# Retention and soft mixture of experts on one core: all stages rebuilt, with steps in pairs, rows of 4 to 8 KB and an order by hand on every engine

## The chip, the cores and the metric

One core of a Trainium2 chip runs the kernel. The metric is the device time of one execution in microseconds (us), lower being better: 169.63 us, the median of 3 runs (169.53 to 170.11). All data are float32.

## The reference

Retention over 4 batches, 8 heads, 768 tokens and head width 64 makes x (3072 x 512). A layer with 8 experts of 4 slots each (`phi` 512 x 32, `w1` 8 x 512 x 1024, `w2` 8 x 1024 x 512) makes the result.

```python
for t in range(S):                                   # retention, scale = 1/8
    state = gamma * state + outer(k[t], v[t])
    y[t] = scale * q[t] @ state
x = y, tokens by (head, width)
logits = x @ phi
d = softmax of logits over all 3072 tokens;  slot_input = d.T @ x
slot_out[e] = relu(slot_input[e] @ w1[e]) @ w2[e]
c = softmax of logits over the 32 slots;     result = c @ slot_out
```

The softmax over all tokens divides the kernel in two: no slot input is known before the last token's logits are.

## The kernel before, in words

**Retention, 24 steps of 128 tokens.** A step is one chunk of one batch, and a batch's six chunks follow each other. `load_kq` and `load_vk` bring a step's keys and queries turned (head width on partitions) and its values and keys untouched, 512 KB each in rows of 4 KB, into slots of one ring of 48. POOL scales the values by a power of gamma (L169). PE makes `scores` (L182, a pair of heads in the two halves of the rows), DVE masks them (L187, four pieces of 256 columns). `attend` adds the products with the carried state (L202) and with the values (L207) in PSUM, and DVE scales the sum into `yT` (L213, four pieces). `state` adds keys times values (L226), and ACT copies the state out (L228). `natural` turns `yT` back on PE (L234; ACT copies, L235). After every fourth step PE makes that group's logits (L245, 32 columns for each of four steps), and in the steps after it `dispatch_p`, `dispatch_u` (L278, L287) and `combine_weights` (L303) run.

**Experts.** After the last group a chain of small operations makes the slot inputs `siT` (L430). `hidden` (L445) multiplies them by `w1` in 16 units of four products, one expert in each quarter of PE's columns; `hidden_t` turns the result. Then L537 multiplies by `w2` in three blocks of 256, 128 and 128 output columns. `finish` copies a block's sum out (L500), spreads it (L504), splits it in two (L506, L507) and multiplies by the combine weights (L519, 512 tokens at a time); DVE and ACT copy the products (L525, L522), and each 512 KB leaves by L523. The blocks before are finished in between the units of the next.

**Order.** PE's order is the program's (`ORDERED`); the other engines are set by the scheduler. SP issues all DMAs on one queue, in program order. Weights are 64 loads of 512 KB: 34 are spread over the 24 steps (`NPRE`), the rest follow as slots come free.

Of the kernel before, what the change touches and what calls it, by code (L numbers as in the profile page):

```python
# [17 lines left out]
C = 128  # L18
# [10 lines left out]
WARM = 5  # L29
# [31 lines left out]
def constants():  # L61
    g = 1.0 - 2.0 ** (-5.0 - np.arange(H, dtype=np.float64))
    p = np.arange(128)
    k = np.zeros((128, K_ALL), np.float64)
    k[:, K_MASK:K_MASK + 128] = p[None, :] >= p[:, None]
    t = (np.arange(NC)[None, :, None] * C + p[:, None, None]).astype(np.float64)
    k[:, K_VSC:K_VSC + 48] = (g[None, None, :] ** -t).reshape(128, 48)
    k[:, K_ID:K_ID + 128] = np.eye(128)
    gp = g[head_of(p[:, None] // 64, np.arange(NPAIR)[None, :])]
    k[:, K_YB:K_YB + 24] = (gp[:, None, :] ** (np.arange(NC)[None, :, None] * C)).reshape(128, 24)  # L70
    k[:, K_J:K_J + GRP] = (p[:, None] // NSLOT) == np.arange(GRP)[None, :]
    k[:, K_YT:K_YT + 64] = (gp[:, :, None] ** (8 * np.arange(16)) / np.sqrt(D)).reshape(128, 64)
# [5 lines left out]
def retention_soft_moe_kernel(  # L78
    ctx: ExitStack,
    tc: tile.TileContext,  # L80
    kq_in: bass.AP,
    vk_in: bass.AP,
    phi: bass.AP,
    w1: bass.AP,
    w2: bass.AP,
    consts: bass.AP,
# [37 lines left out]
    weights = [("w1", 4 * g + j, k) for g in range(2) for k in range(NK) for j in range(4)]  # L124
    for cb, (_, w) in enumerate(BLOCKS):
        for g in range(2):
            if w == 64:
                weights += [("w2", 4 * g + 2 * j, cb) for j in range(2)]
            else:
                weights += [("w2", 4 * g + j, cb) for _ in range(NFC // FPS[w]) for j in range(4)]  # L130

    def load_weights(n):
        for _ in range(n):
            if not weights:
                return
            which, e, k = weights.pop(0)
            t = slot()
            if which == "w1":
                nc.sync.dma_start(t, w1[e, k * 128:(k + 1) * 128, :])
                w1t[e, k] = t  # L140
            else:
                n = 1024 if BLOCKS[k][1] == 64 else FPS[BLOCKS[k][1]] * BLOCKS[k][1]
                nc.sync.dma_start(t[:, 0:n], w2[w2n[0]:w2n[0] + 128 * n].rearrange("(p n) -> p n", n=n))
                w2n[0] += 128 * n
                if BLOCKS[k][1] == 64:
                    w2t[e, k], w2t[e + 1, k] = [t[:, 0:512]], [t[:, 512:1024]]
                else:
                    w2t.setdefault((e, k), []).append(t)

    st = {}  # L150

    def load_kq(i):
        t = slot()
        nc.sync.dma_start(t, kq_in[i])
        st[i] = dict(kT=t[:, 0:512].rearrange("p (g t) -> p g t", t=C),
                     qT=t[:, 512:1024].rearrange("p (g t) -> p g t", t=C))

    def load_vk(i):
        t = slot()
        v = t[:, 0:512].rearrange("p (h e) -> p h e", e=D)  # L160
        st[i].update(v=v, kn=t[:, 512:1024].rearrange("p (h e) -> p h e", e=D))
        if i % NC == NC - 1:
            nc.sync.dma_start(t[:, 0:512], vk_in[i, :, 0:512])
        elif i == 0:
# [4 lines left out]
        nc.gpsimd.tensor_tensor(v, v, vsc[:, i % NC, :].unsqueeze(2).broadcast_to([128, H, D]), ALU.mult)  # L169

    def scores(i):
        s = st[i]
        if i == 0:
            sc = [[ps.tile([128, 2, C], F32, name=n, bufs=2 if n == "sm" else 1) for n in t]
                  for t in (("sc0", "sc1"), ("sm", "sm"))]
        else:
            full = [ps.tile([128, NPAIR, C], F32, name=f"sc{r}") for r in range(2)]
            sc = [[f[:, 2 * hf:2 * hf + 2] for f in full] for hf in range(2)]
# [12 lines left out]

    def attend(i):
        s = st[i]
        c = i % NC
        y = [ps.tile([128, 2, C], F32, name=f"y{b}") for b in range(2)]
        if c > 0:
            for gl in range(2):
                for b in range(2):
                    g = 2 * b + gl
                    for r in range(2):  # L200
                        sl, o = slice(r * D, (r + 1) * D), half_of(r, g) * D
                        nc.tensor.matmul(y[b][o:o + D, gl, :], sst[sl, g, :], s["qT"][sl, g, :],  # L202
                                         start=(gl == 0), stop=False, skip_group_check=True)
        for g in range(NPAIR):
            for r in range(2):
                o = half_of(r, g) * D
                nc.tensor.matmul(y[g // 2][o:o + D, g % 2, :], s["v"][:, 2 * g + r, :], s["A"][:, r, g, :],  # L207
                                 start=(c == 0 and g % 2 == 0), stop=True, skip_group_check=True)
# [21 lines left out]
    def natural(i):  # L230
        s = st[i]
        xp = ps.tile([128, DM], F32, name="xp")
        for g in range(NPAIR):
            nc.tensor.transpose(xp[:, g * 128:(g + 1) * 128], s["yT"][:, g, :], ident)  # L234
        (nc.vector.tensor_copy if i == NSTEP - 1 else nc.scalar.copy)(s["xn"], xp)  # L235
# [13 lines left out]

    def logits(g):  # L250
# [349 lines left out]
```

## Time and profile before

| | |
|---|---|
| time, median of 3 runs | 169.63 us |
| span of the profiled execution | 168.4 us (1.2 us under the median; all sums below start from this execution) |
| PE busy | 153.6 us, 91% |
| DVE, ACT, POOL busy | 93.6, 42.0, 30.5 us |
| moved by DMA | 64.62 MB (64.26 by the kernel's queue), mean 384 GB/s |

The page divides the span in 40 slices. Each shows the busy share of the engines, the clock granted to TensorE (PEclk) and the rate of the DMA engines, so a stage that starves the queue shows as a dip in GB/s. A PE that is "busy" can still be one that works at the pace of its inputs: the chain of waits tells which came last.

### The profile page before, as it was taken

To read this page: it belongs to the slowest core of one execution; us is meant where nothing else is said; L and a number is where in the kernel's file an instruction comes from. 1 tells how busy PE (TensorE), PEld (TensorE's weight loads), DVE (VectorE), ACT (ScalarE), POOL (GpSimd) and SP (SyncE) were. 2 spreads that over 40 slices of the span, in tenths; PEclk is the share of its full clock that TensorE was granted. 3 is DMA by queue.
4 is the path that set the end of the run, shared out by engine and by line. 5 is a ranking of instruction groups with operands and counts; after the bars stand their busy time and mean duration, and the time that the engine had idled before them with its cause. 6 is when DMAs were issued, how large, how long until landed. Compare 5 with 4: busy or idle time off the path is not lost.

```text
span 168.4 us, 5648 instructions
## 1 busy us (share of the span) xinstructions
PE 153.6 (91%) x2370; PEld 109.6 (65%) x2370; DVE 93.6 (56%) x299; ACT 42.0 (25%) x104; POOL 30.5 (18%) x40
## 2 busy tenths in 40 slices
PE   8699779999999999999989799999999999999940
PEld 2577667687868786888678578867432546666620
DVE  0576445596677876694777566984223121355550
ACT  3022213232423141323212232315202030043330
POOL 0252222230304122232223221300050000000000
PEclk9999999999999999999999999999999999999998
DMA  6999999999999999999999999999999999969966
GB/s 185 324 416 411 408 402 415 401 410 406 410 407 406 407 409 406 408 409 404 407 407 411 405 409 406 403 384 367 378 312 404 415 412 406 412 263 397 384 266 263
DMA packets 18458, 64.62 MB, mean 384 GB/s; under 512 B 2048, under 2 KB 2432, under 8 KB 18432
## 3 DMA queue, kind: packets, MB, share of 16 engines
q1 hardware_dynamic: 18432, 64.26, 97.4%
q8 instruction: 19, 0.31, 0.8%
q14 instruction: 7, 0.06, 0.1%
HBM read 57.96 MB, written 6.29 MB: 381 GB/s over the span
## 4 chain that ended last, share of the span: by engine, by line
PE 50%; DMA 40%; DVE 3%; SPq 2%; issue 1%; DVEq 0%
DMA r<-in_kq_dram 18%; DMA r<-in_w_dram 18%; PE sc L537 9%; PE sc L182 6%; PE y L445 4%; PE y L207 4%; DMA r<-in_vk_dram 4%; PE xp L234 3%; PE sm L245 3%; PE y L202 3%; PE xp L445 2%; PE S L445 2%; PE sm L287 2%; PE S L226 2%; PE sm L519 2%; PE sm L331 1%
## 5 line engine op out<-in xcount | busy, mean ns | idle before, releaser
L187 DVE TENSOR_TENSOR r<-sc,kt 128x256 f32<-128x256 f32 x94 | 33.3, 417 | 17.1 <-PE sc L182 16.1
L169 POOL TENSOR_TENSOR r<-r,kt 128x512 f32<-128x512 f32 x24 | 25.1, 1044 | 75.5 <-DMA r<-in_vk_dram 51.1
L213 DVE SCALAR_TENSOR_TENSOR r<-y,kt,ysc 128x128 f32<-128x128 f32 x96 | 27.7, 343 | 9.6 <-PE y L207 6.7
L182 PE MATMUL sc<-r 64*128 64x128 f32 x376 | 27.4, 284 | 4.4 <-DMA r<-in_kq_dram 4.1
L207 PE MATMUL y<-r 128*64 128x128 f32 x384 | 27.3, 280 | 2.6 <-POOL r L169 2.4
L182 PEld LDWEIGHTS sc<-r 64*128 64x128 f32 x376 | 23.1, 187 | 7.3 <-issue 4.0
L207 PEld LDWEIGHTS y<-r 128*64 128x64 f32 x384 | 21.3, 136 | 7.3 <-POOL r L169 3.8
L235 ACT COPY r<-xp 128x512 f32<-128x512 f32 x23 | 13.5, 586 | 42.9 <-PE xp L234 33.3
L234 PE MATMUL xp<-kt,r 128*128 128x128 f32 x96 | 16.5, 287 | 0.1
L537 PE MATMUL sc<-r 128*32 128x128 f32 (+1 forms) x384 | 15.9, 310 | 0.0
L234 PEld LDWEIGHTS xp<-kt,r 128*128 128x128 f32 x96 | 10.6, 141 | 7.0 <-DVE r L187 3.4
L537 PEld LDWEIGHTS sc<-r 128*32 128x32 f32 x384 | 10.6, 110 | 6.0 <-issue 2.9
L228 ACT COPY sst<-S 128x256 f32<-128x256 f32 x20 | 7.5, 373 | 27.6 <-PE S L226 27.5
L202 PE MATMUL y<-r,sst 64*64 64x128 f32 x320 | 13.3, 282 | 0.0
L226 PE MATMUL S<-r 128*64 128x64 f32 x320 | 13.1, 222 | 0.0
L226 PEld LDWEIGHTS S<-r 128*64 128x64 f32 x320 | 12.3, 138 | 0.0
L202 PEld LDWEIGHTS y<-r,sst 64*64 64x64 f32 x320 | 8.5, 132 | 3.3 <-issue 2.1
L445 PE MATMUL y<-r,siT 128*32 128x512 f32 x64 | 8.2, 597 | 0.0
L245 PE MATMUL sm<-r,phis 128*32 128x128 f32 x192 | 7.3, 276 | 0.0
L245 PEld LDWEIGHTS sm<-r,phis 128*32 128x32 f32 x192 | 5.4, 109 | 1.4 <-issue 1.0
L313 POOL TENSOR_TENSOR cnat<-cnat,cz 128x128 f32<-128x128 f32 x6 | 2.4, 401 | 17.5 <-DVE cz L312 14.5
L287 PE MATMUL sm<-r,p 128*32 128x512 f32 x40 | 5.3, 605 | 0.0
(112 smaller groups left out, 124.2 us busy)
## 6 DMA issues: line engine op xcount, KB each, us to landing
r<-in_w_dram SPq DMA_DIRECT2D x64, 512.0 KB, 10.1
r<-in_kq_dram SPq DMA_DIRECT2D x24, 512.0 KB, 10.1
r<-in_vk_dram SPq DMA_DIRECT2D x19, 512.0 KB, 10.1
out_dram<-r SPq DMA_DIRECT2D x12, 512.0 KB, 4.3
r<-in_vk_dram SPq DMA_DIRECT2D x6, 256.0 KB, 9.6
kt<-in_consts_dram SPq DMA_DIRECT2D x1, 136.0 KB, 3.1
kt<-in_consts_dram SPq DMA_DIRECT2D x1, 78.0 KB, 5.6
phis<-in_phi_dram SPq DMA_DIRECT2D x1, 64.0 KB, 6.2
```

What stands on the lines that cost most here:

```text
L169: nc.gpsimd.tensor_tensor(v, v, vsc[:, i % NC, :].unsqueeze(2).broadcast_to([128, H, D]), ALU.mult)
L182: nc.tensor.matmul(sc[g // 2][r][:, g % 2, :], s["kT"][sl, g, :], s["qT"][sl, g, :], start=True, stop=True)
L187: nc.vector.tensor_tensor(A[:, r, 2 * hf:2 * hf + 2], sc[hf][r], mask.unsqueeze(1).broadcast_to([128, 2, C]), ALU.mult)
L202: nc.tensor.matmul(y[b][o:o + D, gl, :], sst[sl, g, :], s["qT"][sl, g, :], start=(gl == 0), stop=False, skip_group_check=True)
L207: nc.tensor.matmul(y[g // 2][o:o + D, g % 2, :], s["v"][:, 2 * g + r, :], s["A"][:, r, g, :], start=(c == 0 and g % 2 == 0), stop=True, sk ...
L213: nc.vector.scalar_tensor_tensor(yT[:, g, :], y[g // 2][:, g % 2, :], ybs[:, c, g:g + 1], ysc[:, g, :], ALU.mult, ALU.mult)
L226: nc.tensor.matmul(S_[r * D:(r + 1) * D, g, :], s["kn"][:, 2 * g + r, :], s["v"][:, 2 * g + r, :], start=(c == 0 and g == 0), stop=True, s ...
L234: nc.tensor.transpose(xp[:, g * 128:(g + 1) * 128], s["yT"][:, g, :], ident)
L235: (nc.vector.tensor_copy if i == NSTEP - 1 else nc.scalar.copy)(s["xn"], xp)
L245: nc.tensor.matmul(q["ltp"][32 * j:32 * j + 32, :], phis[:, p, :], st[GRP * g + j]["yT"][:, p, :], start=(p == 0), stop=(p == NPAIR - 1), ...
L445: nc.tensor.matmul(hp[g][half][32 * j:32 * j + 32, :], siT[:, k, :], w1t[4 * g + j, k][:, half * 512:(half + 1) * 512], start=(k == 0), st ...
L537: nc.tensor.matmul(op[32 * j:32 * j + 32, :w], hT[fc // 4][:, fc % 4, 4 * g + j, :], t[:, f * w:(f + 1) * w], start=(g == 0 and fc == 0), ...
```

## The change

Steps are now ordered chunk by chunk with the four batches inside, and worked off in 12 pairs P, step 2P and step 2P+1, so that consecutive steps share no state; there are four states (`sst`). Each step's inputs are one tile and one load: 1 MB in rows of 8 KB (`FULL`, 12 steps), or 768 KB in rows of 6 KB (`LEAN`, 11 steps) without the untouched keys, which PE makes from the turned ones (`turn_k`, 8 steps in `TURNED`) or which are not needed (the last four). Step 0 and all constants come as two loads of 512 KB in rows of 4 KB; mask and identity are made by POOL. Weights are 1 MB loads in rows of 8 KB; `PACE` says how many go ahead of a pair's inputs. The buffers are 13 large ones for weights, 6 for inputs, which take weights when the inputs are through, and a ring of 9 of 4 KB.

The decay from chunk to chunk is put into the queries by POOL (`decay_q`, L212), so the carried state needs no scaling and DVE adds to it (L297). Masks and copies out of PSUM are 512 columns wide; ACT takes half of the `yT` copies. The combine weights are turned by DVE in place of PE, and are no longer split in two: the last product (L650) takes 32 rows and 384 tokens, four of them in the four quarters of PE's rows. An output transfer is 768 KB in rows of 6 KB. `hidden` takes the halves of the hidden columns one after the other. All engines keep the program's order. Step 0's values are scaled in three pieces.

```diff
-ORDERED = {mybir.EngineType.PE}
-NPRE = 34
-NRING = 48
+ORDERED = "all"
+NBIG = 13
+NIN = 6
+NRING = 9
+PACE = (1, 1, 1, 2, 1, 2, 1, 2, 2, 0, 2, 2)
+TURNED = (0, 1, 2, 3, 4, 8, 12, 14)
+LEAN = [i for i in range(1, NSTEP) if i in TURNED or i >= NSTEP - B]
+FULL = [i for i in range(1, NSTEP) if i not in LEAN]
...
+    def load_in(i):
+        t = large(inp)
...
+            nc.sync.dma_start(t[:, 0:1024], first_[0])
+            nc.sync.dma_start(first, first_[1])
...
+            nc.sync.dma_start(t[:, 0:1536], in3[LEAN.index(i)])
...
+            nc.sync.dma_start(t, in4[FULL.index(i)])
+
+    def turn_k(i, name):
+        kp = bank(name)
+        for g in range(NPAIR):
+            nc.tensor.transpose(kp[:, g * 128:(g + 1) * 128], st[i]["kT"][:, g, :], ident)
+        nc.scalar.copy(st[i]["kn"], kp.rearrange("p (h d) -> p h d", d=D))
+
+    def decay_q(i):
+        q = st[i]["qT"]
+        if i >= B:
+            nc.gpsimd.tensor_tensor(q, q, qtab, ALU.mult)
...
+        nc.scalar.copy(y[:, :, 0:2, :], pr[P]["Y"][0])
+        nc.vector.tensor_copy(y[:, :, 2:4, :], pr[P]["Y"][1])
...
+    for P in range(NPP):
+        last = P == NPP - 1
+        g = P // 2
+        load_weights(PACE[P])
+        if 2 * P + NIN < NSTEP:
+            load_in(2 * P + NIN)
+            load_in(2 * P + NIN + 1)
         else:
+            weight_pool[0] = inp
         if not last:
+            for i in (2 * P + 2, 2 * P + 3):
+                decay_q(i)
+            if P % 2 == 0 and 0 < P < NPP - 2:
+                next_chunk()
+            for i in (2 * P + 2, 2 * P + 3):
+                decay_v(i)
...
+        carry_mm(P)
         if last:
+            dispatch_u(g - 1, ["A0"])
+            logits_mm(g, (0, 1))
+            load_halves(2)
+            load_weights(2)
+        attend_mm(P)
         if last:
+            load_halves(1, sall)
+            break
+        attend_copy(P)
+        if P < NPP - B // 2:
+            state_mm(P)
+            state_add(P)
+        if 2 * P + 2 in TURNED:
+            turn_k(2 * P + 2, "A0")
+        natural_mm(P)
+        natural_copy(P)
+        if P % 2 == 0 and P > 0:
+            turn_mm(g - 1)
+            turn_copy(g - 1)
+        if P % 2 == 1:
+            if g > 0:
+                dispatch_u(g - 1, ["S"])
+            logits_mm(g, range(GRP))
...
+        score_mm(2 * P + 2)
+        score_mask(2 * P + 2)
+        score_mm(2 * P + 3)
+        score_mask(2 * P + 3)
...
-                    nc.tensor.matmul(cp[0:mw], s4r[:, m * 128:m * 128 + mw],
-                                     c4T[q].bitcast(F32R)[:, half * 512:(half + 1) * 512], start=True, stop=True)
+                    nc.tensor.matmul(cp, s4[32 * j:32 * j + 32, m * 128:(m + 1) * 128],
+                                     cT[32 * j:32 * j + 32, 3 * h:3 * h + 3, :], start=True, stop=True,
+                                     skip_group_check=True, tile_position=(32 * j, 0))
```

**SP's queue in the middle of retention.** Before (about two and a half steps; `in_kq`, `in_vk` are a step's inputs, `in_w` weights):

```order
L139 DMA r<-in_w_dram 128x1024 x2
L154 DMA r<-in_kq_dram 128x1024
L168 DMA r<-in_vk_dram 128x1024
L139 DMA r<-in_w_dram 128x1024
L154 DMA r<-in_kq_dram 128x1024
L163 DMA r<-in_vk_dram 128x512
```

After (pairs 2 to 4, up to the inputs of step 14; `in_x` is a step's one input tile):

```order
L163 DMA b<-in_w_dram 128x2048
L201 DMA b<-in_x_dram 128x2048 x2
L163 DMA b<-in_w_dram 128x2048 x2
L199 DMA b<-in_x_dram 128x1536
L201 DMA b<-in_x_dram 128x2048
L163 DMA b<-in_w_dram 128x2048
L199 DMA b<-in_x_dram 128x1536
```

Inputs are asked for six steps ahead, and the wait for a free buffer stands once in a pair, in front of the first of its two inputs.

**PE in a step, and in a pair.** Before, from a step's carried products to its turn (`S` state, `sc` scores, `xp` turned output):

```order
L207 MATMUL y_297<-r 64x128 x4
L207 MATMUL y_298<-r 64x128 x4
L226 MATMUL S<-r 64x64 x8
L182 MATMUL sc_334<-r 128x128
L182 MATMUL sc_335<-r 128x128
L182 MATMUL sc_334<-r 128x128
L182 MATMUL sc_335<-r 128x128
L182 MATMUL sc_334<-r 128x128
L182 MATMUL sc_335<-r 128x128
L182 MATMUL sc_334<-r 128x128
L182 MATMUL sc_335<-r 128x128
L234 MATMUL xp<-kt,r 128x128 x4
```

After, pair 4 (`Y` the sums, `A` scores and turned output, L364 the turn of the group's exponents):

```order
L260 MATMUL Y_656<-r,b 64x128 x4
L260 MATMUL Y_657<-r,b 64x128 x4
L260 MATMUL Y_656<-r,b 64x128 x4
L260 MATMUL Y_657<-r,b 64x128 x4
L288 MATMUL S<-b 64x64 x16
L304 MATMUL A_712<-mi,r 128x128 x4
L304 MATMUL A_717<-mi,r 128x128 x4
L364 MATMUL sm<-mi,pT 128x128
L227 MATMUL A_729<-b 128x128
L227 MATMUL A_730<-b 128x128
```

The next scores moved behind the turn of the same pair's output; between the products with the values and that turn only the pair's state is left.

**PE at the end.** Before, from the last units of the last block:

```order
L537 MATMUL sc_2222<-r 32x128 x24
L504 MATMUL y_2318<-os,rep 128x128
L519 MATMUL sm<-r 128x512
L519 MATMUL S<-r 128x512
L519 MATMUL sm<-r 128x512
L519 MATMUL xp<-r 128x512
L519 MATMUL y_2339<-r 128x512
L519 MATMUL sm<-r 128x512
```

After:

```order
L669 MATMUL A_2012<-b,r 32x128 x32
L638 MATMUL Y_2111<-os,rep 128x128
L650 MATMUL S<-cT,r 128x384
L650 MATMUL sm<-cT,r 128x384
L650 MATMUL A_2119<-cT,r 128x384
L650 MATMUL Y_2121<-cT,r 128x384
L650 MATMUL A_2129<-cT,r 128x384
L650 MATMUL A_2131<-cT,r 128x384
L650 MATMUL A_2133<-cT,r 128x384
L650 MATMUL Y_2135<-cT,r 128x384
```

Six products of 512 tokens into three outputs became eight of 384 tokens into two, in eight different banks.

## Rows read from the trace of the kernel before

**Rows 1.** From the page: the span, PE, the rate in 40 slices of 4.21 us, the kernel's DMA queue (packets, MB, share of 16 engines' span), and what was read and written.

```profile
span 168.4 us, 5648 instructions
PE 153.6 (91%) x2370; PEld 109.6 (65%) x2370; DVE 93.6 (56%) x299; ACT 42.0 (25%) x104; POOL 30.5 (18%) x40
GB/s 185 324 416 411 408 402 415 401 410 406 410 407 406 407 409 406 408 409 404 407 407 411 405 409 406 403 384 367 378 312 404 415 412 406 412 263 397 384 266 263
DMA packets 18458, 64.62 MB, mean 384 GB/s; under 512 B 2048, under 2 KB 2432, under 8 KB 18432
q1 hardware_dynamic: 18432, 64.26, 97.4%
```

**Rows 2.** Stretches of the span: its length, busy us of PE, PEld, DVE, ACT, POOL (with instructions), granted clock as a share of 2.4 GHz, DMA share, GB/s.

```profile
0.00:4.00 4.00, 3.23 (x9) 1.04 (x10) 0.00 (x0) 1.28 (x1) 0.20 (x4) 1.00 0.57 186
4.00:8.00 4.00, 2.38 (x34) 1.84 (x34) 2.11 (x5) 0.00 (x0) 1.04 (x1) 1.00 0.99 313
20.00:40.00 20.00, 18.65 (x326) 14.99 (x314) 12.82 (x45) 5.34 (x15) 4.69 (x6) 1.00 1.03 407
80.00:100.00 20.00, 18.23 (x317) 14.62 (x313) 13.67 (x48) 5.28 (x16) 5.26 (x6) 1.00 1.03 408
110.00:130.00 20.00, 20.00 (x209) 10.41 (x213) 8.75 (x27) 5.26 (x16) 2.18 (x3) 1.00 0.99 366
145.00:166.00 21.00, 16.43 (x278) 10.78 (x266) 10.54 (x21) 6.62 (x12) 0.00 (x0) 1.00 0.87 344
166.00:168.40 2.40, 0.00 (x0) 0.00 (x0) 0.00 (x0) 0.00 (x0) 0.00 (x0) 0.78 0.40 159
```

**Rows 3.** The chain that ended last, in retention: start, us, what (x counts instructions; a product is two of them, a turn one).

```profile
42.03 1.01 PE sm L245 x32
...
46.48 0.99 PE sm L287 x8
47.47 0.59 PE xp L234 x4
48.06 0.60 PE y L202 x16
48.66 1.02 PE y L207 x16
49.68 0.46 PE S L226 x16
50.15 1.09 PE sc L182 x16
51.24 0.26 PE sm L303
51.50 0.44 PE xp L234 x4
```

**Rows 4.** The same chain from the last logits to the end.

```profile
111.91 1.85 PE sm L245 x32
...
119.32 1.00 PE xp L445 x8
120.31 0.86 PE y L445 x8
...
138.95 6.40 PE sc L537 x128
...
157.75 1.49 PE sc L537 x48
...
159.61 0.50 PE y L504 x2
...
160.13 0.30 DVE r L506
```

**Rows 5.** The timeline's start and end: start, us, engine, instructions, and the idle time before with what ended it.

```profile
4.35 0.71 PE L182 MATMUL sc<-r 64*128 64x128 f32 x8
...
6.04 1.04 POOL L169 TENSOR_TENSOR r<-r,kt 128x512 f32<-128x512 f32 x1 [5.60 <-DMA r<-in_vk_dram]
...
148.52 15.36 SPq L523 DMA_DIRECT2D out_dram<-r  x12
...
159.26 0.29 DVE L500 COPY os<-sc 128x128 f32<-128x128 f32 x1 [1.02 <-PE sc L537]
```

**Rows 6.** Loads of the later weights: ns of issuing, and first and last start; and for all weights and for the outputs the time from issue to landing.

```profile
L143 SPq DMA_DIRECT2D r<-in_w_dram x32: 327/328/1449, 99.2 to 139.5; - x32
DMA to landing us min/median/max: 4.9/10.1/11.4
DMA to landing us min/median/max: 2.9/4.3/6.0
```

**Rows 7.** Groups of instructions: out<-in, shapes, count | busy us, mean ns | idle us before and what ended it.

```profile
L187 DVE TENSOR_TENSOR r<-sc,kt 128x256 f32<-128x256 f32 x94 | 33.3, 417 | 17.1 <-PE sc L182 16.1 <-issue 0.8
L169 POOL TENSOR_TENSOR r<-r,kt 128x512 f32<-128x512 f32 x24 | 25.1, 1044 | 75.5 <-DMA r<-in_vk_dram 51.1 <-PE sc L182 17.2 <-PE S L226 4.4
L235 ACT COPY r<-xp 128x512 f32<-128x512 f32 x23 | 13.5, 586 | 42.9 <-PE xp L234 33.3 <-issue 7.1 <-DMA r<-in_w_dram 2.5
L525 DVE COPY r<-sm 128x512 f32<-128x512 f32 x5 | 3.4, 687 | 1.6 <-PE sm L519 1.6
L213 DVE SCALAR_TENSOR_TENSOR r<-y,kt,ysc 128x128 f32<-128x128 f32 x96 | 27.7, 343 | 9.6 <-PE y L207 6.7 <-PE S L226 2.3 <-POOL cnat L313 0.5
```

More of the change, by code (lines that the diff above doesn't have):

```diff
@@ L135, in load_weights @@
                 return
[L136 to L137 removed]
+            which, *at = weights.pop(0)
+            t = large(weight_pool[0])
             if which == "w1":
[L139 to L148 removed]
+                nc.sync.dma_start(t, w1[tuple(at)])
+                w1t[tuple(at)] = t
+            else:
+                nc.sync.dma_start(t, w2[w2n[0]])
+                w2n[0] += 1
+                take(at, [t[:, 0:1024], t[:, 1024:2048]])
@@ new lines, in take, with load_halves @@
+    def take(at, tiles):
+        w = BLOCKS[at[0]][1]
+        for t, fcs in zip(tiles, halves_of(*at)):
+            for x, (e, fc) in enumerate(fcs):
+                w2t[e, at[0], fc] = t[:, x * w:(x + 1) * w]
+    def load_halves(n, first_half=None):
+        for _ in range(n):
+            _, *at = weights.pop(0)
+            tiles = [first_half if first_half is not None else slot(), slot()]
+            for h in range(2):
+                nc.sync.dma_start(tiles[h], w2[w2n[0], :, h * 1024:(h + 1) * 1024])
+            take(at, tiles)
+            w2n[0] += 1
@@ L171, in scores @@
-    def scores(i):
-        s = st[i]
[L173 to L178, printed above, removed]
+                     qT=t[:, 512:1024].rearrange("p (g t) -> p g t", t=C),
+                     v=t[:, 1024:1536].rearrange("p (h e) -> p h e", e=D),
@@ L200, in attend @@
                     for r in range(2):
[L201 to L208, printed above, removed]
@@ L230, in natural @@
[L230 to L235, printed above, removed]
-    gs = {}
+                        nc.tensor.matmul(p["y"][k][b][half(half_of(r, g)), gl, :], sst[(2 * P + k) % B][half(r), g, :],
+                                         s["qT"][half(r), g, :], start=(gl == 0 and (k == 0 or P == NPP - 1)),
+                                         stop=False, skip_group_check=True)
@@ new lines, in state_mm, with state_add @@
+    def state_mm(P):
+        S_ = pr[P]["S"] = bank("S").rearrange("p (i g e) -> p i g e", i=2, e=D)
+        for k in range(2):
+            s = st[2 * P + k]
+            for g in range(NPAIR):
+                for r in range(2):
+                    nc.tensor.matmul(S_[half(r), k, g, :], s["kn"][:, 2 * g + r, :], s["v"][:, 2 * g + r, :],
+                                     start=True, stop=True, skip_group_check=True)
+    def state_add(P):
+        for k in range(2):
+            d = sst[(2 * P + k) % B]
+            if P < B // 2:
+                nc.scalar.copy(d, pr[P]["S"][:, k])
+            else:
+                nc.vector.tensor_tensor(d, d, pr[P]["S"][:, k], ALU.add)
@@ new lines, in combine_c, with warm @@
+    def combine_c(g):
+        nc.vector.transpose(cT[:, g, :], gs[g]["cn"].rearrange("p a s -> p (a s)"))
+    def warm(n, name="sm", w=WN):
+        wp = bank(name)
+        for _ in range(n):
+            nc.tensor.matmul(wp[0:WM, 0:w], nc.const_aps.tensor(0.0, [128, WM], WDT),
+                             nc.const_aps.tensor(0.0, [128, w], WDT), start=True, stop=True)
+    first = slot()
+    load_in(0)
+    ones = nc.const_aps.tensor(1.0, [128, C], F32)
+    for m, op in ((mask, ALU.is_ge), (ident, ALU.is_equal)):
+        nc.gpsimd.affine_select(m, ones, [[1, C]], op, 0.0, base=0, channel_multiplier=-1)
@@ new lines, in retention_soft_moe_kernel @@
+    nc.scalar.copy(kt, first[:, 0:K_ALL])
+    load_in(1)
+    load_in(2)
+    load_in(3)
+    for i in range(4, NIN):
+        load_in(i)
+    decay_v(0, first[:, K_VSC:K_VSC + 48].rearrange("p (c h) -> p c h", h=H), ((0, 2), (2, 4), (4, H)))
+    decay_v(1)
+    warm(WARM)
+    score_mm(0)
+    score_mask(0, 2)
+    carry_mm(0)
+    turn_k(0, "S")
+    warm(1)
+    attend_mm(0, [0])
+    score_mm(1)
+    score_mask(1)
+    decay_table(ytab, K_YT)
+    turn_k(1, "sm")
+    for P in range(NPP):
[5 more added lines that the diff above has]
+            load_in(2 * P + NIN + 1)
+        else:
+            weight_pool[0] = inp
@@ new lines, in retention_soft_moe_kernel @@
+    natural_copy(NPP - 1, ks=(0,))
+    logits_mm(g, (2, 3))
+    natural_mm(NPP - 1, (1,))
+    logits(g)
+    nj = small("nj", [128, GRP])
+    nc.vector.tensor_scalar(nj, kt[:, K_J:K_J + GRP], nmc[:, 1:2], None, ALU.mult)
+    natural_copy(NPP - 1, ("vector", "vector"), (1,))
+    warm(2, "A0", 128)
+    dispatch_p(g)
+    mb = bank("S", (128, GRP))
+    nc.tensor.matmul(mb, rep, nj, start=True, stop=True)
+    al = gs[g]["al"] = small("al", [128, 1])
+    nc.scalar.activation(al, gs[g - 1]["m"], AF.Exp, bias=nmc[:, 1:2], scale=1.0)
@@ new lines, in retention_soft_moe_kernel, with hidden @@
+    turn_l(g)
+    combine_c(g - 1)
+    combine_a(g)
+    hp = [bank(n) for n in ("A2", "Y0")]
+    hs = slot()
+    def hidden(hf, g, k):
+        for j in range(4):
+            a = g * NK * SIW + k * SIW + 4 * j
+            nc.tensor.matmul(hp[hf][32 * j:32 * j + 32, :], si0[:, a:a + NSLOT],
+                             w1t[hf, g, k][:, j * 512:(j + 1) * 512],
+                             start=(g == 0 and k == 0), stop=(g == 1 and k == NK - 1), skip_group_check=True,
+                             tile_position=(0, 32 * j))
+        if g == 1 and k == NK - 1:
+            h = hs[:, hf * 512:(hf + 1) * 512]
+            nc.scalar.copy(h[:, 0:256], hp[hf][:, 0:256])
+            nc.vector.tensor_copy(h[:, 256:512], hp[hf][:, 256:512])
@@ new lines, in retention_soft_moe_kernel @@
+    for cb, (c0, w) in enumerate(BLOCKS):
+        if cb == len(BLOCKS) - 1:
+            n_co[0] = 0
+        op = bank(("A0", "A1")[cb % 2])
+        units = ([(g, 4 * hf + f) for hf in range(2) for g in range(2) for f in range(4)] if cb == 0 else
+                 [(g, fc) for g in range(2) for fc in range(NFC)])
+        for n, (g, fc) in enumerate(units):
+            for j in range(4):
+                nc.tensor.matmul(op[32 * j:32 * j + 32, :w], hT[fc // 4][:, fc % 4, 4 * g + j, :],
+                                 w2t[4 * g + j, cb, fc], start=(n == 0), stop=(n == len(units) - 1),
+                                 skip_group_check=True, tile_position=(0, 32 * j))
+            if cb == 0 and n == 2:
+                hidden_t(1)
+            for f in pend:
+                next(f, None)
```

614 lines of the change are left out of this document (296 added, 318 removed).

## The prediction

> **What bounds the kernel now.** I read the page first. PE is busy for 91% of the span, and the queue moves 64.62 MB at a mean of 384 GB/s; both look full [rows 1]. The slices part them: from the third to the 25th the rate lies between 401 and 416 GB/s, and it falls at the start, in slices 26 to 30, and from slice 36 on [rows 1]. So the queue flows at one rate as long as it is given work. Two long stretches fix that rate at 407 and 408 [rows 2]. At 408 the 64.62 MB need 158.4 us; the span is 168.4. The other 10.0 us are found stretch by stretch [rows 2], each as its length times the shortfall against 408:
> - start: 186 for 4 us is as if nothing flowed for 2.2 us; then 313 for 4 us loses 0.9 (small constants, step 0's inputs in pieces).
> - 110 to 130 us: 366, so 2.1 us.
> - 145 to 166 us: 344, so 3.3 us.
> - after the last byte: 159 for 2.4 us are 0.9 us of flow, so 1.5 us at the end.
>
> The chain says why. In retention it changes between loads and PE, which is at 0.91 to 0.93 of the span there [rows 2]: the queue sets the pace. A step on PE is 1.09 (scores), 0.60, 1.02, 0.46 and 0.44 to 0.59 (turn), about 3.67 us; logits cost 1.01 and the two dispatch pieces 0.99 and 0.26 in each group of four [rows 3]. From the last logits at 111.9 PE sets the pace [rows 4]. The last weights are asked for at 139.5 and can land 4.9 us later [rows 6], but the first output is not ready before 148.5 [rows 5], and the queue runs short. The kernel is bound by the queue, with 6.3 us of gaps (0.9 + 2.1 + 3.3) that PE's lateness and the small first loads cause.
>
> **The change, part by part.**
>
> *Bytes.* Inputs were 24 x 0.5 MiB of keys and queries, and 11 MiB of values and keys. Now step 0 and the constants are 1 MiB, 12 steps 1 MiB, 11 steps 0.75 MiB: 21.25 MiB. With 32 of weights and 6 of output that is 59.25 MiB or 62.13 MB, against 64.26 [rows 1]. The 0.36 MB of other traffic stays: 62.49 MB. Saved: 2.13 MB, 5.2 us at 408.
>
> *Rate.* No row shows 6 and 8 KB rows. Bounds are the lowest and highest slice of the flat part, 401 and 416 [rows 1]; the nearest rows are the long stretches at 407 and 408 [rows 2], of 4 KB rows. Since most bytes now come in rows twice as long, I go a little up from there, to 411: 1.1 us. The Trainium skill speaks against more: its page "DMA: Bandwidth & Descriptors", section "iDMA fabric", gives 408.7 GB/s for a stream of 1 MiB loads in 4 KiB rows. The trace agrees (408 with loads half as large), so by it larger loads alone bring nothing, and the time would be 157.8.
>
> *Start.* The first keys and queries are the same 512 KB and land at 4.35 [rows 5], so the 2.2 us stay. Every row is now 4 KB or more: I count the 0.9 us as saved. Values and constants are one load that ends at 1.05 MB of the queue, 2.2 + 2.6 + 0.85 (the lag of the first load: 4.35 against 2.2 + 1.3) = 5.6; before, POOL started at 6.04 [rows 5]. Mask and identity on POOL have no row; between 0.3 and 1.0 us each they end before 4.35.
>
> *Does PE keep up in retention?* A pair is 2 x 3.67 = 7.34 us. Even pairs add 0.26, odd ones 1.01 and, from P=3, 0.99; turning a step's keys is four turns, 0.44. Step 5 lands when 5 MiB are through: 2.2 + 12.9 + 0.85 = 15.9; with POOL's 1.04 [rows 7] and the scores' 1.09, pair 2 starts at 18.0. From there PE's own sum is 7.6, 9.8, 7.6, 9.8, 8.0, 9.3, 7.6, 9.3 for pairs 2 to 9 (turned keys of 8, 12, 14 in pairs 3, 5, 6), so pair 10 starts at 87. The last inputs end at 34.25 MiB, 35.9 MB: 88 + 2.2 + 0.85 = 91. Pair 10 (no state) takes 6.7, so its last scores follow at about 93.5 by either reckoning; the last pair's products (1.2, 0.99, 0.5, 2.04) end at 98.6, against 111.9 before. Retention is thus balanced between PE and queue, and 13 us shorter, since fewer bytes stand ahead of the last inputs.
>
> *Other engines there.* POOL: 24 scalings stay, 20 of queries and 4 of the table are added at 1.044 [rows 7]: 50 us of 95; in a pair 4 or 5 us of 8. DVE: 48 masks of 512 columns at 0.69 for 96 at 0.417; 12 copies at 0.69 for 96 scalings at 0.343; 20 state adds at 0.42 [rows 7]: 50 us for 73. ACT takes 12 copies of 0.59. DVE's turns of 128 columns have no row; at 0.15 to 0.7 each, twelve are at most 8 us. All lie beside PE. If that cover failed, PE would wait in each pair: the third rival.
>
> *Does the queue run dry in between?* Ahead of the hidden stage it is given 34.25 + 2 + 2 + 2 + 2 + 1 = 43.25 MiB, the last of them when pair 11's products free their buffers at 98.6. They keep it busy until 2.2 + 111.2 = 113.4. The later ones wait for w1 buffers. From the last products' end to the hidden stage took 7.4 us (111.9 to 119.3, [rows 4]); I keep it, since the same small operations stand in that chain. So hidden starts at 106.0, frees 1 MiB each 0.86 us [rows 4] and the queue takes 2.6 us for each: it never waits. PE has 6.5 us of slack here (113.4 less 106.9). The 2.1 us go.
>
> *End.* Hidden: 16 x 0.86 to 119.9. Block 0: 16 units of 256 columns, half as long as the 0.86 of 512, and some turns, to 127.5. Blocks of 128 columns take 16 x 0.25 (48 instructions, six units, in 1.49, [rows 4]). All loads end at 2.2 + 136.9 = 139.1 (53.25 MiB), 140 with the lag. Block 1 runs from 127.5 to 136 with block 0's four outputs at 0.9 each; block 2's second half needs the last load: 140 to 142.1. Behind it stand 0.3, 0.5, 0.3 (no second split, [rows 4]), four products (below) and two copies of 0.6 on either engine: outputs at 146 and 147. The queue has 3 MiB of block 0 and 1.5 of block 1 to carry until 150.7, so it does not wait for them. The 3.3 us go, the 1.5 at the end stays.
>
> *Sum.* 168.4 - 5.2 - 0.9 - 2.1 - 3.3 - 1.1 = 155.8, or the other way 2.2 + 62.49/0.411 + 1.5 = 155.7. The median of the runs lies 1.2 above the profiled span: **157.0 us**. At 401 it is 160.7, at 416 155.1.
>
> **Rivals.**
>
> *Long rows flow faster.* For it: the flat part's slices differ by 2% upwards with 4 KB rows already, so the engines can take more than 408. Against: no slice is above 416 [rows 1]. I let 8 KB rows go as far above that slice as it is above the flat rate, to 424: 62.49/0.424 + 3.7 + 1.2 = 152.3 us. Chance 0.12. The same page of the Trainium skill has 425 GB/s for one 16 MB load (section "Bandwidth"); no run here shows it.
>
> *Quarter rows do not run together.* Eight outputs, each of four such products, need it: an instruction of 512 columns takes 0.43 alone if four quarters of columns share 0.86 for eight [rows 4], so one of 384 takes 0.32 and a product 0.64. Four at once cost 0.64 per output, one after the other 2.56. Halves of rows run only partly together: the scores' 16 instructions of 128 columns take 1.09 where turns of 128 columns take 0.11 each, a factor of 1.6 [rows 3]. Without any overlap PE ends block 1 at 142, block 2 at 152, and asks for the last output at 160; from that request to the end of the span were 4.5 us before (163.9 to 168.4, [rows 5, 1]): 165.7 us. It decides from about 1.5 us per output, where the 3.7 us between PE's last output (147) and the queue (150.7) are used up. Chance 0.07. The Trainium skill ("TensorE: Matmul & The Clock Gate", Part 3) gives 3.07 times for four row tiles; by that it is 0.83 per output, and hidden.
>
> *PE waits in every pair, and the kernel gets slower.* All engines now keep the program's order, and the next scores stand behind the turn of the output. If in each of ten pairs one round of copies is exposed (0.69 on DVE, two of 0.586 on ACT, POOL's 1.044, [rows 7]: 2.9 us), PE is 29 us late; 6.5 are slack, so the time is 179. It beats the old kernel from 6.5 + 12.6 = 19 us on, 1.9 per pair. Against: 0.92 of state stands between products and turn, 1.2 of carried products between scores and masked scores, and steps of a pair share no state. Chance of slower 0.04; of the same at 0.7 to 1.5 us per pair, 160 to 166 us, 0.10.
>
> **How the numbers follow.** The forecast, the queue that never runs dry at 401 to 416, has 0.66. Range 152.2 to 161.5: it takes in the forecast with both its bounds, the faster rows, and the mildest part of the third rival, about 0.8. A run of this kernel can tell 0.3%, 0.5 us, from no change. Faster 0.95, within 0.01, slower 0.04.
>
> **What would show it.** Right: 62.1 MB on the kernel's queue; a flat rate of 408 or a little more with no dip between 15 us and the end of the outputs; the last products of retention near 99 us, hidden near 106, last weights landing near 140, PE's last output product some 7 us before the queue ends. Wrong: a rate of 420 and more (first rival); output products of over 1.5 us per output, with the queue idle behind 145 us (second); PE waiting for DVE, ACT or POOL in each pair, retention past 106 us and a dip near 113 (third).

## The result and the profile after

The changed kernel takes 158.47 us (median of 4 runs, 158.41 to 158.59), the kernel before 169.75 (169.53 to 170.11): a ratio of 0.9335, 95% interval 0.9321 to 0.9349. The forecast was 157.0. The profiled run has a span of 156.6 and a time of 158.46. One of the four runs of `e4_lean_all` below (160.05) was in a slower state and is left out there, which makes its gain 0.7 us where a later expectation has 0.6.

The page of the changed kernel: span, PE, rates in 40 slices of 3.92 us, packets, the kernel's queue, and the shares of the chain that ended last.

```profile
span 156.6 us, 5485 instructions
...
PE 144.9 (93%) x2412; PEld 107.7 (69%) x2412; DVE 78.8 (50%) x187; ACT 42.1 (27%) x100; POOL 58.7 (38%) x67
...
GB/s 154 423 424 420 416 412 423 416 414 420 405 421 413 417 414 416 416 421 414 407 419 414 416 396 404 410 382 425 410 428 423 414 423 412 418 417 415 373 373 116
DMA packets 9816, 62.48 MB, mean 399 GB/s; under 512 B 1088, under 2 KB 1088, under 8 KB 4544
...
q1 hardware_dynamic: 9792, 62.13, 96.8%
...
PE 92%; DVE 2%; issue 1%; DVEq 0%
```

The same shares of the kernel before:

```profile
PE 50%; DMA 40%; DVE 3%; SPq 2%; issue 1%; DVEq 0%
```

Against [rows 1], half as many packets move 2.13 MB less, and the two deep dips (312 and 263) are gone. What remains is 382 near 104 us, 373 twice between 145 and 153, and the last slice. The chain is PE almost throughout, where loads had 40% of it before. That alone doesn't show that PE holds the end: relieving PE brings nothing (`e3_no_turns` below).

Stretches of the changed kernel (columns as in [rows 2]):

```profile
0.00:4.00 4.00, 3.16 (x8) 0.88 (x8) 0.00 (x0) 1.28 (x1) 0.74 (x6) 1.00 0.50 158
4.00:20.00 16.00, 16.00 (x231) 13.82 (x230) 8.87 (x16) 5.61 (x13) 8.49 (x10) 1.00 1.02 421
20.00:40.00 20.00, 20.00 (x411) 17.71 (x413) 11.71 (x25) 6.03 (x14) 14.38 (x17) 1.00 1.01 416
...
100.00:105.00 5.00, 5.00 (x67) 3.91 (x67) 3.08 (x11) 2.08 (x7) 0.40 (x1) 1.00 1.03 392
...
110.00:120.00 10.00, 10.00 (x96) 3.04 (x88) 1.09 (x4) 1.19 (x2) 0.22 (x1) 1.00 1.02 418
...
145.00:150.00 5.00, 2.60 (x38) 1.29 (x30) 2.53 (x6) 1.63 (x4) 0.00 (x0) 1.00 0.85 352
...
152.00:153.00 1.00, 0.00 (x0) 0.00 (x0) 0.00 (x0) 0.00 (x0) 0.00 (x0) 0.52 0.99 412
153.00:154.00 1.00, 0.00 (x0) 0.00 (x0) 0.00 (x0) 0.00 (x0) 0.00 (x0) 0.50 0.65 264
154.00:155.00 1.00, 0.00 (x0) 0.00 (x0) 0.00 (x0) 0.00 (x0) 0.00 (x0) 0.50 0.19 80
```

The 313 of the second stretch [rows 2] is gone, the flat rate is 416 to 418 for 407 and 408, and PE is at 1.00 of most stretches of retention for 0.91 to 0.93. At the end the DMA share falls in steps (0.99, 0.65, 0.19).

The timeline: start of step 0's scores, POOL's pieces, the carried products of pairs 2 and 10 (L251), the first turn of the last pair's output (L304), the hidden products (L589), block 0 (L669), the ends of blocks 1 and 2 (DVE L634) with an output of block 1 between them, and the last outputs' first products (L650).

```profile
4.36 1.58 PE L227 MATMUL A<-b 64*128 64x128 f32 x16
...
5.67 1.33 POOL L217 TENSOR_TENSOR r<-r 128x128 f32<-128x128 f32 x3 [4.23 <-DMA r<-in_first_dram]
...
23.11 1.10 PE L251 MATMUL Y<-b,sst 64*64 64x128 f32 x32
...
89.01 1.10 PE L251 MATMUL Y<-b,sst 64*64 64x128 f32 x32
...
101.42 0.66 PE L304 MATMUL A<-mi,r 128*128 128x128 f32 x4
...
107.69 2.78 PE L589 MATMUL A<-b,qtab 128*32 128x512 f32 x24
...
122.17 0.39 PE L669 MATMUL A<-b,r 128*32 128x256 f32 x2
...
139.17 0.29 DVE L634 COPY os<-A 128x128 f32<-128x128 f32 x1
...
140.72 0.58 PE L650 MATMUL sm<-cT,r 32*128 32x384 f32 x1
...
145.60 0.29 DVE L634 COPY os<-A 128x128 f32<-128x128 f32 x1 [1.26 <-PE A L669]
...
146.82 0.58 PE L650 MATMUL S<-cT,r 32*128 32x384 f32 x1 [0.38 <-DVE r L639]
146.83 0.58 PE L650 MATMUL sm<-cT,r 32*128 32x384 f32 x1
146.84 0.58 PE L650 MATMUL A<-cT,r 32*128 32x384 f32 x1
146.84 0.58 PE L650 MATMUL Y<-cT,r 32*128 32x384 f32 x1
```

Scores start where they did [rows 5], the hidden products 11.6 us earlier than before (119.3, [rows 4]): nearly the whole gain of 11.8 us in the span is there by the end of retention. The last four rows are products in the four quarters of PE's rows, which start within 20 ns and end together.

The kernel's issues: the later weights, and the outputs (columns as in [rows 6]); and what the inputs' loads (L201) waited for (us in total, times, longest).

```profile
L166 SPq DMA_DIRECT2D b<-in_w_dram x13: 327/328/903, 92.9 to 119.7; - x13
L656 SPq DMA_DIRECT2D out_dram<-b x8: 332/332/348, 134.0 to 149.8; - x8
...
SPq L201 <- PE S L288: 28.9, 5, 8.2
```

The last weights are asked for at 119.7, not at 139.5 [rows 6]; the last output at 149.8, 6.8 us before the end of the span. An input's load waits for a buffer that PE frees with the state's products (L288).

### The profile page after: what moved, and what is told of

Same layout as the page of the kernel before. It is cut to its first block, busy times and chain, and to the rows that moved or that the text cites. A ratio compares the mean times of both kernels' runs of the same rounds, so it can differ in the third digit from the quotient of the medians.

```text
span 156.6 us, 5485 instructions
## 1 busy us (share of the span) xinstructions
PE 144.9 (93%) x2412; PEld 107.7 (69%) x2412; DVE 78.8 (50%) x187; ACT 42.1 (27%) x100; POOL 58.7 (38%) x67
## 2 busy tenths in 40 slices
DMA packets 9816, 62.48 MB, mean 399 GB/s; under 512 B 1088, under 2 KB 1088, under 8 KB 4544
## 3 DMA queue, kind: packets, MB, share of 16 engines
q1 hardware_dynamic: 9792, 62.13, 96.8%
## 4 chain that ended last, share of the span: by engine, by line
PE 92%; DVE 2%; issue 1%; DVEq 0%
PE A L227 16%; PE Y L260 15%; PE A L669 9%; PE A L304 7%; PE Y L251 6%; PE S L288 6%; PE Y L589 4%; PE A L589 4%; PE sm L328 4%; PE sm L424 3%; PE S L384 3%; PE A L206 2%; PE sm L650 2%; PE S L650 1%; PE Y L650 1%
## 5 line engine op out<-in xcount | busy, mean ns | idle before, releaser
L235 DVE TENSOR_TENSOR r<-A,mi 128x512 f32<-128x512 f32 (+1 forms) x50 | 30.1, 662 | 22.5 <-PE A L227 22.5
L212 POOL TENSOR_TENSOR b<-b,qtab 128x512 f32<-128x512 f32 x20 | 25.5, 1278 | 21.5 <-DMA b<-in_x_dram 17.4
L227 PE MATMUL A<-b 64*128 64x128 f32 x384 | 25.6, 282 | 0.0
L227 PEld LDWEIGHTS A<-b 64*128 64x128 f32 x384 | 22.9, 191 | 3.1 <-issue 2.0
L217 POOL TENSOR_TENSOR b<-b,kt 128x512 f32<-128x512 f32 x23 | 23.7, 1049 | 2.2 <-DMA b<-in_x_dram 2.2
L260 PE MATMUL Y<-r,b 128*64 128x128 f32 x352 | 22.5, 276 | 0.5 <-issue 0.5
L260 PEld LDWEIGHTS Y<-r,b 128*64 128x64 f32 x352 | 19.2, 137 | 2.9 <-issue 2.6
L669 PE MATMUL A<-b,r 128*32 128x128 f32 (+1 forms) x336 | 15.9, 300 | 0.0
L669 PEld LDWEIGHTS A<-b,r 128*32 128x32 f32 x336 | 10.3, 110 | 6.4 <-issue 4.4
L311 ACT COPY r<-A 128x512 f32<-128x512 f32 x23 | 12.4, 592 | 7.5 <-PE A L304 7.5
L304 PE MATMUL A<-mi,r 128*128 128x128 f32 x96 | 13.3, 278 | 0.4 <-ACT r L279 0.3
L288 PE MATMUL S<-b 128*64 128x64 f32 x304 | 11.1, 222 | 0.9 <-issue 0.9
L304 PEld LDWEIGHTS A<-mi,r 128*128 128x128 f32 x96 | 10.4, 141 | 1.7 <-ACT r L279 0.6
L288 PEld LDWEIGHTS S<-b 128*64 128x64 f32 x304 | 10.4, 138 | 0.5 <-issue 0.5
L251 PE MATMUL Y<-b,sst 64*64 64x128 f32 x304 | 10.6, 276 | 0.0
L251 PEld LDWEIGHTS Y<-b,sst 64*64 64x64 f32 x304 | 8.2, 132 | 1.2
L297 DVE TENSOR_TENSOR sst<-sst,S 128x256 f32<-128x256 f32 x16 | 6.0, 417 | 3.0 <-PE S L288 3.0
```

What stands on the lines that cost most here:

```text
L212: nc.gpsimd.tensor_tensor(q, q, qtab, ALU.mult)
L217: nc.gpsimd.tensor_tensor(v, v, vsc[:, i // B, a:b].unsqueeze(2).broadcast_to([128, b - a, D]), ALU.mult)
L227: nc.tensor.matmul(s["sc"][r][:, g, :], s["kT"][half(r), g, :], s["qT"][half(r), g, :], start=True, stop=True, skip_group_check=True)
L235: nc.vector.tensor_tensor(s["A"][:, r, g:g + n], s["sc"][r][:, g:g + n], mask.unsqueeze(1).broadcast_to([128, n, C]), ALU.mult)
L251: nc.tensor.matmul(p["y"][k][b][half(half_of(r, g)), gl, :], sst[(2 * P + k) % B][half(r), g, :], s["qT"][half(r), g, :], start=(gl == 0 a ...
L260: nc.tensor.matmul(pr[P]["y"][k][g // 2][half(half_of(r, g)), g % 2, :], s["v"][:, 2 * g + r, :], s["A"][:, r, g, :], start=(P < B // 2 an ...
```

## The experiments

Theory: PE's row of work and the queue's bytes are **level**, each just reaching the end of the span; the gain came from letting both run without a gap. Rival A: the queue alone holds the end, as predicted. Rival B: PE alone does. Microseconds worse or better are against the changed kernel's 158.47; the ratios are to the kernel before, timed beside each run (169.71 to 169.88).

**Work moved between the two.** The list of steps whose keys PE turns, 4 or 12 long instead of 8:

```diff
-TURNED = (0, 1, 2, 3, 4, 8, 12, 14)
+TURNED = (0, 1, 2, 3)                              # e1_turn4
+TURNED = (0, 1, 2, 3, 4, 6, 8, 10, 12, 14, 16, 18) # e2_turn12
```

> Keys of steps 4, 8, 12 and 14 are loaded again in place of being turned by PE: the queue carries 1.05 MB more (2.5 us at the 416 GB/s of the changed kernel's trace), PE does four turns of 0.59 us less (2.4 us). If the queue alone sets the time: 158.5 + 2.5 = 161.0 us. If PE alone sets it: 158.5 - 2.4 = 156.1. If the two are level (the queue's gaps of about 0.7 us before the hidden stage and 0.8 at the end are all that PE costs): the gaps close and the bytes cost, 159.5 to 160.

> The other way: steps 6, 10, 16 and 18 are turned by PE as well, so the queue carries 1.05 MB less (2.5 us) and PE does 2.4 us more. Queue alone: 156.0 us. PE alone: 160.9. Level: PE's 2.4 us come out nearly whole, 160 to 161, and the queue runs dry before the hidden stage and at the end.

Measured: with 4 turned 160.67 us (ratio 0.9458, 0.944 to 0.9476), with 12 turned 161.73 (0.9519, 0.9484 to 0.9554); 2.2 and 3.3 us worse than 8. Both are above what the level theory had (159.5 to 160, 160 to 161). With 4 the time is near the queue's own 161.0: that PE had less to do brought nearly nothing. With 12 the hidden products start at 111.95, 4.3 us later than with 8, for 2.4 us of turns; PE also stood still for 1.0 and 1.3 us near 86 and 94, where the profile names no cause, and the queue ran short:

```profile
95.00:100.00 5.00, 4.64 (x69) 3.87 (x63) 1.13 (x5) 2.47 (x7) 1.62 (x3) 1.00 0.55 187
```

Two neighbours, later:

```diff
+TURNED = (0, 1, 2, 3, 4, 8, 12)          # e9_turn7
+TURNED = (0, 1, 2, 3, 4, 8, 10, 12, 16)  # e10_turn9
```

> One step's keys fewer are turned on PE (7 instead of 8): the queue has 0.26 MB more (0.64 us), PE 0.6 us less. If PE and the queue are level at 8, the time rises by up to 0.64 us, to 158.6 to 159.1. If PE alone holds the end at 8 steps (its last outputs are late by 1.4 us of an idle queue), it falls, to 157.9 to 158.3.

> Two changes of the list: step 14 is not turned, and steps 10 and 16 are, so 9 instead of 8 steps: the queue has 0.26 MB less (0.64 us), PE 0.6 us more. If they are level at 8, the time rises by 0.5 to 0.9 us, to 158.9 to 159.4 (a line from 158.47 at 8 to 161.73 at 12 gives 159.3). If the queue alone holds the end, it falls to 157.8 to 158.3.

Measured: 158.79 (0.9358, 0.9336 to 0.9381) and 159.74 (0.9418, 0.9399 to 0.9437). So 160.67, 158.79, **158.47**, 159.74, 161.73 for 4, 7, 8, 9, 12: time rises on both sides, where either rival alone would have given a slope of one sign. From 7 down to 4 each step costs about its 0.64 us of queue, from 9 up to 12 about its 0.59 us of PE's turns. Where between 7 and 9 the lowest point lies is not shown: the intervals of 7 and 8 overlap, 9 missed its forecast (158.9 to 159.4), and in the profiled runs of 7 and 9 step 1's values came 1.3 us later than with 8, in a stretch where the three programs are alike:

```profile
7.63 1.04 POOL L217 TENSOR_TENSOR b<-b,kt 128x512 f32<-128x512 f32 x1 [0.62 <-DMA b<-in_x_dram]
...
8.91 1.04 POOL L217 TENSOR_TENSOR b<-b,kt 128x512 f32<-128x512 f32 x1 [2.02 <-DMA b<-in_x_dram]
...
8.89 1.04 POOL L217 TENSOR_TENSOR b<-b,kt 128x512 f32<-128x512 f32 x1 [2.13 <-DMA b<-in_x_dram]
```

(8, 7 and 9 turned.) Pair 2 then starts at 24.05 and 24.02 for 23.11, so up to 0.9 us of both differences to 8 may be this start; its cause is not shown. Between 7 and 9, which share it, two turned steps cost 0.95 us.

**Relief of one, of the other, of both.**

```diff
 def turn_k(i, name):                                  # e3_no_turns: PE relieved
-    kp = bank(name)
-    ... (four turns and a copy)
+    st[i]["kn"] = st[i]["kT"].rearrange("p g (b d) -> p (g b) d", d=D)
...
-        nc.sync.dma_start(t, in4[FULL.index(i)])      # e4_lean_all: queue relieved
+        nc.sync.dma_start(t[:, 0:1536], in4[FULL.index(i)])
+        st[i]["kn"] = st[i]["kT"].rearrange("p g (b d) -> p (g b) d", d=D)
```

> PE alone is relieved: no keys are turned (the state of the eight steps is made from the keys as they were loaded), same loads. PE does 8 x 0.59 = 4.7 us less, the queue carries the same 62.1 MB. PE alone sets the time: 153.8 us. Queue or level: at most the gaps of 0.7 and 0.8 us go, 157.0, and the rate is flat up to the last output.

> The queue alone is relieved: no step's untouched keys are loaded (the state of the twelve steps is made from the turned keys as they were loaded), PE does the same. The queue carries 3.15 MB less, 7.6 us. Queue alone: 150.9 us. PE alone or level: PE's last outputs stay where they are, near 149 us of the span, and only the outputs waiting ahead of them are gone: 156.5 to 158; the queue shows long gaps.

> Both limits are relieved at once: no step's keys are turned on PE (PE has 4.7 us less) and none is loaded untouched (the queue has 3.15 MB, 7.6 us, less); the state's and dispatch products use the keys as they stand, so their numbers are not the reference's. If PE and the queue are level and each alone holds the end, the time falls by about PE's 4.7 us, far more than the 0.1 and 0.6 us which either part brought alone: 153.5 to 155 us. If a third thing holds the end (the first load's delay, the order of loads, the tail of outputs), it stays at 157 to 158.

`e8_both` has both edits. All three leave work out: they make states from turned keys, so their results are not the reference's; e3 and e8 also leave out ACT's copies of the turned keys, for which PE hardly waits in the changed kernel (0.3 us for ACT in all).

Measured: PE relieved 158.36 (0.9321, 0.9298 to 0.9343), queue relieved 157.78 (0.9284, 0.926 to 0.9308), both 152.41 (0.8984, 0.8955 to 0.9012). The parts alone bring 0.1 and 0.7 us, together 6.1: the level theory holds, and gives more than the 4.7 expected. The forecast for e3 (157.0) failed: PE's last outputs came 2 us earlier, and most of the gap in the queue from 145 to 150 us closed (400 GB/s for 352), but the time did not fall. Its end:

```profile
145.00:150.00 5.00, 1.18 (x16) 0.41 (x8) 1.95 (x4) 1.63 (x4) 0.00 (x0) 0.99 0.97 400
...
151.00:152.00 1.00, 0.00 (x0) 0.00 (x0) 0.00 (x0) 0.00 (x0) 0.00 (x0) 0.50 0.73 301
152.00:153.00 1.00, 0.00 (x0) 0.00 (x0) 0.00 (x0) 0.00 (x0) 0.00 (x0) 0.50 0.53 221
153.00:154.00 1.00, 0.00 (x0) 0.00 (x0) 0.00 (x0) 0.00 (x0) 0.00 (x0) 0.50 0.34 141
154.00:155.00 1.00, 0.00 (x0) 0.00 (x0) 0.00 (x0) 0.00 (x0) 0.00 (x0) 0.50 0.13 55
```

The queue ends over four us, its share falling in steps: I read this as DMA engines that finish one after another, the slowest last. `e1_turn4`, whose queue had no gap either, ends in the same way (0.84, 0.57, 0.48, 0.18, 0.06). The rows of e2, whose queue ran short just before its end (PE was 4.3 us later), show the other case:

```profile
152.00:153.00 1.00, 0.66 (x10) 0.04 (x4) 0.97 (x3) 0.93 (x3) 0.00 (x0) 1.00 0.67 277
153.00:154.00 1.00, 0.00 (x0) 0.00 (x0) 0.98 (x3) 0.70 (x2) 0.00 (x0) 1.00 0.49 203
...
155.00:156.00 1.00, 0.00 (x0) 0.00 (x0) 0.00 (x0) 0.00 (x0) 0.00 (x0) 0.94 1.02 406
156.00:157.00 1.00, 0.00 (x0) 0.00 (x0) 0.00 (x0) 0.00 (x0) 0.00 (x0) 0.50 0.96 399
157.00:158.00 1.00, 0.00 (x0) 0.00 (x0) 0.00 (x0) 0.00 (x0) 0.00 (x0) 0.50 0.75 295
```

After a dry spell the share stays high to the last us. This would explain why a gap near the end costs little and closing it gains little: the engines that lag would use it to catch up. It is argued, not shown: the rows have no share of a single DMA engine.

**Where the rate comes from.** Rows of 4 KB for the weights, in the same 1 MB loads:

```diff
-                nc.sync.dma_start(t, w1[tuple(at)])
+                nc.sync.dma_start(t.rearrange("p (h n) -> p h n", h=2), w1[tuple(at)].rearrange("h p n -> p h n"))
```

> Only the layout of the weights in DRAM is changed: each 1 MB load still fills a tile of 128 x 2048 numbers with one DMA, but its rows in DRAM are 4 KB instead of 8. Inputs and outputs stay. If the rows' length gives the rise from 408 to 416 GB/s, the windows that hold weights alone (105 to 140 us) fall to about 408, 33.6 MB of weights then take 1.6 us longer, and the time is 159.5 to 160.5 us. If it comes from larger loads or fewer of them, the rate stays at 415 to 418 and the time at 158.3 to 158.7.

Measured: 160.04 (0.9428, 0.9409 to 0.9448), 1.6 us slower. A stretch of weights alone (the next 10 us have 408 too):

```profile
110.00:120.00 10.00, 10.00 (x96) 3.17 (x92) 1.44 (x6) 1.92 (x3) 0.40 (x1) 1.00 1.02 408
```

408 for the 418 of the changed kernel at the same place, and the same as before, whose loads were half as large [rows 2]: the length of the rows gives the rise, the size of the loads nothing. The Trainium skill has 408.7 for 1 MiB loads in 4 KiB rows ("DMA: Bandwidth & Descriptors", "iDMA fabric"); the 408 here agrees.

**First values in one piece.**

```diff
-    decay_v(0, first[...].rearrange("p (c h) -> p c h", h=H), ((0, 2), (2, 4), (4, H)))
+    decay_v(0, first[...].rearrange("p (c h) -> p c h", h=H))
```

> The first values are scaled in one instruction of 128 x 512 instead of three pieces. The first products then wait for a whole scaling of 1.04 us (the row of the trace for step 1) instead of a first piece of about 0.44, so PE starts them at about 7.2 instead of 6.97 and is late by 0.2 to 0.6 us. If PE and queue are level, that costs at most as much at the end: 158.5 to 159.0 us. If POOL's piecing brings nothing, or saves in sum (three pieces take 1.33), 158.3 to 158.5.

Measured: 158.34 (0.9331, 0.9311 to 0.9351): nothing that can be told. This part of the change brings nothing.

**Only PE in the written order.**

```diff
-ORDERED = "all"
+ORDERED = {mybir.EngineType.PE}
```

> Only PE keeps the order in which the program is written; DVE, ACT, POOL and the DMA queue are left to the scheduler. If the written order of the other engines matters (a copy or a load that is put behind another one), PE waits for ACT, DVE or POOL, its end moves out by 1 us or more, and the time is 159.5 us or above. If PE's order alone carries the gain, 158.2 to 158.8 us.

Measured: 161.76 (0.9526, 0.9506 to 0.9547), 3.3 us slower. DVE and PE in pair 2 of this kernel, and the start of pair 10:

```profile
24.08 1.10 PE L251 MATMUL Y<-b,sst 64*64 64x128 f32 x32
...
24.37 1.28 DVE L235 TENSOR_TENSOR r<-A,mi 128x512 f32<-128x512 f32 x2
25.56 0.60 DVE L414 TENSOR_SCALAR cz<-cz 128x4 f32<-128x4 f32 x1
25.70 1.09 PE L260 MATMUL Y<-r,b 128*64 128x128 f32 x14 [0.15 <-DVE r L235]
...
26.29 1.26 DVE L235 TENSOR_TENSOR r<-A,mi 128x512 f32<-128x512 f32 x2
27.10 1.48 PE L260 MATMUL Y<-r,b 128*64 128x128 f32 x15 [0.31 <-DVE r L235]
...
93.58 1.10 PE L251 MATMUL Y<-b,sst 64*64 64x128 f32 x32
```

and in the changed kernel:

```profile
22.32 2.48 DVE L235 TENSOR_TENSOR r<-A,mi 128x512 f32<-128x512 f32 x4 [3.63 <-PE A L227]
...
24.15 1.97 PE L260 MATMUL Y<-r,b 128*64 128x128 f32 x32
```

The scheduler put small steps of the combination between the masks, and PE's products, 1.97 us in one piece, were spread over 25.1 to 28.7: 1.6 us lost in this pair, and 3.6 in pairs 2 to 9 (69.5 us for 65.9). The written order of the other engines carries part of the gain, and keeps out a mild form of the third rival's wait. The run frees DVE, ACT, POOL and the queue at once; the lines show DVE's part, the others' are not parted.

Of the kernels that compute the whole reference none is faster than the changed one beyond what can be told.

## Why the prediction was right, and where it was not

The time came out in the range for the main reason given: fewer bytes, and a queue that hardly stops. That the queue alone would hold the end, with PE some us ahead, was wrong: PE is level with it.

- **Bytes** (5.2 us): right; 62.13 MB were moved.
- **Rate** (411): the flat rate was mis-sized, 416 to 418, the upper bound of the range; for weights e5 shows why. But the price of a byte is not the flat rate. From 2.5 us (0 to 4 us at 158 against 416) to the last packets, at about 155.0, the 62.48 MB went at 410. So 411 came out near by luck, through two misses: a flow 5 GB/s faster and an end 1.3 us longer.
- **Start**: the 0.9 went (421 from 4 us on); 2.5 for the 2.2 that stay.
- **PE in retention**: the step that failed. Pair 2 was to start at 18.0, from the landing of step 5, with PE's own sum only from there. But PE's work up to there runs without a break from 4.36 to 23.11: I never added it up. Pairs were shorter than priced (pairs 2 to 9 in 65.9 us for 69.1), so pair 10 began at 89.0 for 87, the last products ended near 101.5 for 98.6, and hidden began at 107.7 for 106.0 (6.2 us behind them for 7.4). The 6.5 us of slack were counted at the hidden stage only. But the loads ahead of it wait for buffers that PE frees, so a PE that was later starved the queue well before: with 12 turned it moved 187 GB/s from 95 to 100 us.
- **Middle gap** (2.1): went nearly; 90 to 105 us still lose about 0.7 (392 in its last third).
- **End**: the last weights were early, as said. But PE took 37.9 us from hidden to the end of block 2 (107.7 to 145.6), not the 34.2 of my terms (13.9 + 7.6 + 8.5 + two halves of 2.1), so nothing waited for the last load, the outputs were issued at up to 149.8, and 145 to 150 us lost 0.8 us of queue. Most of the miss is block 2: 6.4 us (139.17 to 145.60) for 4.2, since block 1's two outputs are made in it (from 140.72) and no term had them. (My own terms also put the last outputs at 145 and 146, not at the 146 and 147 written.) Of the 3.3, 2.5 went. After the last full us the ragged end costs 2.8 for my 1.5.
- **Sum**: 155.7 for 156.6 of span. Start +0.3, rate -1.8, gaps +1.5, end +1.3 make +1.3; the few stretches above 416 give 0.4 back. The time lies 1.9 above the span for 1.2 assumed: the other 0.7 of the 1.5 missed.
- **Rivals**: quarter rows run together, 8 instructions of an output in about 0.8 us (two outputs from 146.82 to 148.40), for 0.64 if fully together and 2.56 if not. The Trainium skill's 3.07 times ("TensorE: Matmul & The Clock Gate", Part 3), by which it was 0.83, agrees roughly. Long rows are faster, but by 2%, not 4. PE's waits in every pair stay out; e7 shows a mild form, 161.8. That this lies in the 160 to 166 given to it is luck: by my own terms (ten pairs, less 6.5 of slack) 0.7 to 1.5 us per pair made 157.5 to 165.5, and e7 is 4.6 us late at pair 10 (1.0 from its start, 0.45 per pair). The 6.5 of slack should have taken all of that up; 3.3 reached the end.

## What to carry to other kernels

When an edit removes one limit, add up the other engine's whole row of work from its first instruction, not from where the old limit let it start: two limits that come out level must be relieved together (here 0.1 and 0.7 us alone, 6.1 both). Price a queue that never stops by bytes over the time to its last packet (410 GB/s here), not by its flat rate (416 to 418). If an engine's order is written by hand, keep the small side work of its feeders behind what it waits for.

## What the hardware showed that I had not expected

- 1 MB loads of weights flow at 418 GB/s from rows of 8 KB and at 408 from rows of 4 KB.
- A queue without a gap before its end ended over 4 to 5 us, its DMA share falling in steps (e3: 0.73, 0.53, 0.34, 0.13); one that had just run dry (e2) stayed at 0.96 and more until 157 us and had moved everything by 158.
- POOL's product of two full operands takes longer than that with one of them repeated along the row. Groups of the changed kernel (columns as in [rows 7]):

```profile
L212 POOL TENSOR_TENSOR b<-b,qtab 128x512 f32<-128x512 f32 x20 | 25.5, 1278 | 21.5 <-DMA b<-in_x_dram 17.4 <-DVE qtab L136 3.6 <-PE S L384 0.5
L217 POOL TENSOR_TENSOR b<-b,kt 128x512 f32<-128x512 f32 x23 | 23.7, 1049 | 2.2 <-DMA b<-in_x_dram 2.2
```

I had priced both at 1.044; the 0.23 us more lay beside PE.
